# First rows turned in four operations, first weights in halves, two warming matmuls less, last output rows in halves

## The chip, the core and the metric

The kernel runs on one core of a Trainium2 chip. The metric is the time of one execution on the device in microseconds (us). The span is what the profiler sees from the first to the last event on the core; the time of the execution lies a little above it. Engines are named as the profile names them: PE is TensorE, PEld its weight loads, DVE VectorE, ACT ScalarE, POOL GpSimd, SP the engine whose queue issues the DMAs.

## What is computed

The output is a gated mix of two blocks on the same input x (2048 rows of 512): `g * a + (1 - g) * b`, with one gate `g` for each row.

```python
g = sigmoid((x * gate_w).sum(-1, keepdims=True))
# A: 64 segments of 32 rows, one after the other; 8 memory rows go ahead of each
h = concatenate([mem, xs])                       # 40 rows
q, k, v = h @ Wq, h @ Wk, h @ Wv                 # 32 heads of 128
o = softmax(mask(q @ k.T * scale)) @ v @ Wo      # 40 rows of 512
mem, a_s = o[:8], o[8:]                          # the memory of the next segment, the output rows
# B: 4 spans of 512 rows, 32 heads of 16
b = (sig(beta) * phi(q) @ M / (phi(q) @ z) + (1 - sig(beta)) * causal_softmax(q, k, v)) @ wo
M, z = M + phi(k).T @ v, z + phi(k).sum()        # after each span
```

Since A's memory goes from segment to segment, its 64 segments are a serial chain; B's work is put between their steps.

## The kernel before, in words

The program is a list of operations for each engine (class `Prog`). Each engine works through its list in order; an operation names what it reads and writes, and waits on the semaphores of the operations that it depends on. PSUM has eight banks, handed out by `Banks` from a list of free ones, a bank being a resource of its own (`rbank`): an operation that reads a bank waits for the whole operation that wrote it. DMAs are issued by SP in the order of its own list, so an entry that waits holds up those behind it.

**The head.** `plan_warm` (L500) gives TensorE 9 matmuls of 128x512 on zeros (`WARM`, L12). `plan_loads` (L515) issues, in this order: x 0 (rows 0 to 511, two DMAs of 256 rows), B's wk, wq and wv (512 KB, a DMA each), x 1, beta and mem0, x 2, x 3, gate_w. The 12 DMAs of A's weights Wk, Wq and Wv come later, one after every third piece of B's projections, between the stores of these pieces. x lies for the time being in the memory of A's Wo (`Wo_sb` in the profile), and wv in `woB_sb`.

`x_chunk` (L576) turns 512 rows of x to put the contraction on the partitions. For each half of 256 rows it takes one bank, and one operation makes 8 transposes of 128x128 (L588); two copies then take the bank to `xT`, on ScalarE for the first half and on VectorE for the second (`evac`, L390 and L392). `b_projections` makes the pieces of B: `pk` (L679) is a projection of k or q, four matmuls of 128x512 over the four parts of the contraction (L686), `kn` turns k (L720), `pv` makes v (L704), `mz` adds to the state M and z (L738). Results are stored in DRAM scratch (L662: `scr_kqd`, `scr_vd`, `scr_mzd`), from where B's attention loads them again. The memory of the head's tensors is used again for A's; `over` (L368) collects which earlier operations a tensor of A must wait for. One such case is `t1_sb`, which lies over `V17` and first holds late V rows of B (L841, then a copy by ScalarE, L390).

**The middle.** A's segments and B's attention follow 16 lists of unit names written out by hand (`A_LIST0` to `A_LIST15`, four segments each). A unit's name says what it does: `3.W1a` is a product with Wo in the fourth segment of the list, `H0` and `H1` copy the two halves of the product's sum to `WF`, `F0` and `F1` add up (fold) the four row groups and turn them by matmuls against a 0/1 matrix (L1396), `ax0` and `ax1` copy the folded rows to `aT_st`. A `~` behind a name exchanges ScalarE and VectorE for that unit's copy.

**The output rows.** `tail_units` (L1468) makes the output of 128 rows (a group; there are 16): `tb` multiplies B's rows by wo (16 matmuls of 128x512 in quarters of the partitions, L1487), `tbe` scales them by 1 - g on ScalarE into `t1_sb` (L1495), `tf` and `tfe` add g times A's rows on VectorE (L1520) and store the result (L1522). For the last group, A's rows are turned by 16 matmuls against the identity (`atr`, L1511), and sum and store are made in two halves. `tl` in a list calls `tail_load` (L1755), which sets up the next group; it does so only once that group's rows of A are all written (`stored`). So the last group's units all come after the last list, in the loop at the end of `plan_a`.

Of the kernel before, what the change touches and what calls it, by code (L numbers as in the profile page):

```python
# [8 lines left out]
F32 = mybir.dt.float32  # L9

DEV = dict(nseg_limit=None)
WARM = 9  # L12


class Op:
# [242 lines left out]
def build(nc, es, A_x, A_mem0, A_Wq, A_Wk, A_Wv, A_Wo, B_wq, B_wk, B_wv, B_wo, B_beta, gate_w, out, dbg=None):  # L258
# [109 lines left out]
    def over(home):  # L368

        parts = {"mem0_sb": "mem0", "beta_sb": "beta", "gB_sb": "gB", "omgB_sb": "omgB"}  # L370
        ops = []
        for p in v.under[home]:
            p = parts.get(p, p)
            for n, r in list(R.items()):
                if n == p or p in ("V17", "phK") and n.startswith(p) or p.startswith("stgk") and n[:-1] == p:
                    ops += ([r.w] if r.w else []) + r.readers
        return list({id(o): o for o in ops}.values())
    G = {}
# [136 lines left out]
def plan_loads(v, A_x, A_mem0, A_Wq, A_Wk, A_Wv, B_wq, B_wk, B_wv, B_wo, B_beta, gate_w):  # L515
# [8 lines left out]
            o = 4 * k + 2 * h  # L524
            ld("x%d%d" % (k, h), v.x_sb[:, o:o + 2, :], xsrc[:, o:o + 2, :], "x_sb%d%d" % (k, h), "dma_x%d%d" % (k, h))
    x(0)
    for nm, dst, src in (("wk", v.wkB, B_wk), ("wq", v.wqB, B_wq), ("wv", v.wvB, B_wv)):
        ld("b" + nm, dst[:, :, :].rearrange("p (h n) m -> p h (n m)", h=2), src.rearrange("(h p n) m -> p h (n m)", h=2, n=2), nm + "B", "dma_" + nm)
    x(1)
    g = P.group("small")  # L530
    for fn, res in ((lambda s: s.dma_start(v.beta_sb[:, :], B_beta.rearrange("(o n) -> o n", o=1).to_broadcast([128, v.HB])), "beta"),
# [44 lines left out]
def x_chunk(v, k):  # L576

    P, Rs, BK, C = v.P, v.Rs, v.BK, v.C
    for h in range(2):
        bk = BK.take()  # L580
        tiles = (4 * k + 2 * h, 4 * k + 2 * h + 1)

        def f(pe, bk=bk, tiles=tiles):
            ins = None
            for n, i in enumerate(tiles):
                for c in range(C):
                    o = (n * C + c) * 128
                    ins = pe.transpose(v.pb16[bk][:, o:o + 128], by_pairs(v.x_sb[:, i, :])[:, c, :], v.ident[:, :])  # L588
            return ins
        P.op("pe", f, reads=[Rs("x_sb%d%d" % (k, h)), Rs("ident")], writes=[v.rbank[bk]], name="xtr%d_%d" % (k, h))  # L590
        t0 = 128 * tiles[0]
        dst = v.xT[:, :, t0:t0 + 256].rearrange("p c (n t) -> p n c t", t=128)
        src = v.pb16[bk][:, 0:1024].rearrange("p (n c t) -> p n c t", n=2, c=C)
        for n in range(2):
            v.evac("dve" if h else "act", dst[:, n, :, :], src[:, n, :, :], [bk], [Rs("xT%d_%d%d" % (k, h, n))], "xev%d_%d%d" % (k, h, n))
        BK.give(bk)


def x_res(v, k):
# [49 lines left out]
def b_projections(v):  # L649
# [29 lines left out]
    def pk(sb, f, m):  # L679
        w, wr = (v.wkB, "wkB") if m == "k" else (v.wqB, "wqB")  # L680
        bk = BK.take()

        def fp(pe):
            ins = None
            for c in range(C):
                ins = pe.matmul(v.pb[bk], w[:, c, f * 128:(f + 1) * 128], v.xT[:, c, 512 * sb:512 * (sb + 1)], start=(c == 0), stop=(c == C - 1))  # L686
            return ins
        P.op("pe", fp, reads=x_res(v, sb) + [Rs(wr)], writes=[v.rbank[bk]], name="p%s%d_%d" % (m, sb, f))
        stage = v.stgk[f][:, "kq".index(m), :]
        rs = Rs("stgk%d%s" % (f, m))  # L690
        v.evac("dve" if m == "k" and f < 3 else "act", stage, v.pb[bk], [bk], [rs], "ev%s%d_%d" % (m, sb, f))
        BK.give(bk)
        if m == "k":
            return
        store("stk%d_%d" % (sb, f), v.kqd[sb, f], v.stgk[f][:, :, :], [Rs("stgk%dk" % f), rs], [Rs("kqd%d_%d" % (sb, f))], "stk%d_%d" % (sb, f), "stk%d" % f)
# [159 lines left out]
class BAttn:  # L855
# [394 lines left out]
    2.V0x 2.V0y 2.v1 2.Y0 2.n1 2.M0 2.N1 2.PV1 2.v0~ 2.L0 2.PL1 2.E1a 2.E1b tb 2.N0 2.PV0 2.n0 2.PL0 2.E0b 2.W1a tbe tf 2.W1b 2.W0b 2.E0a~ 2.W0a 2.oL pl0x  # L1250
    2.H0 2.H1 2.F0 2.hm0 pl0 2.F1 2.hm1 3.K0x tfe 3.Q0x 2.ax0~ 3.Q0y 3.q0~ 3.K0y 3.k0 3.TQ0 3.K1x 3.K1y 3.Q1x tl 3.Q1y 3.TK0 3.S0 3.V0x 3.k1~ 3.q1 3.TK1
    3.X0 3.TQ1 pl1x 3.V0y 3.Y0 3.S1 3.M0 2.ax1 3.X1 tb 3.v0 3.Y1 3.L0 3.n0 tbe 3.V1x 3.M1 tf 3.N0 tfe 3.L1 3.n1 3.N1 3.PV0 3.PL0 3.E0b~ 3.E0a 3.V1y 3.v1~
    pl1 pl1e 3.W0a 3.PV1 3.PL1 3.W0b pf 3.E1b~ 3.W1b 3.E1a pfe~ 3.W1a 3.H0~ 3.H1~ tb 3.F0 3.ax0~ tbe 3.F1 3.ax1 tf tfe
    """
A_LISTS = (A_LIST0,) + (A_LIST1,) + (A_LIST2,) + (A_LIST3,) + (A_LIST4,) + (A_LIST5,) + (A_LIST6,) + (A_LIST7,) + (A_LIST8,) + (A_LIST9,) + (A_LIST10,) + (A_LIST11,) + (A_LIST12,) + (A_LIST13,) + (A_LIST14,) + (A_LIST15,)
A_ENG = dict(E0a="act", E0b="act", E1a="act", E1b="dve", H0="act", H1="act", K0="act", K1="act", KL0="dve", KL1="dve", O0="dve", O1="dve",
# [4 lines left out]
def plan_a(v, nseg):  # L1261
# [146 lines left out]
    def ol_units(g):  # L1408
# [40 lines left out]
        def turn():  # L1449
            stored.append(g)  # L1450
            flat = aT_st[par][:, :, :].rearrange("p c t -> p (c t)")
            turned = [Rs("aTl%d" % par)] + [Rs("aTx%d_%d" % (par, r)) for r in range(4)]
            P.op("dve", lambda d: d.transpose(flat.bitcast(F32), flat.bitcast(F32)), writes=turned, name="aT%d" % g)
            grp = P.group("as%d" % g, "as%d" % par)
            rows = v.aTd[g].rearrange("(b t) (h j i) -> j t h b i", b=4, h=2, j=4)
            for j in range(4):
                P.dma(grp, lambda sp, j=j: sp.dma_start(rows[j], flat[SEG * j:SEG * (j + 1), :].rearrange("p (h b i) -> p h b i", h=2, b=4)),
                      reads=turned, writes=[Rs("aTd%d" % g)], name="sta%d_%d" % (g, j))
# [9 lines left out]
    def tail_units(g):  # L1468

        last = g == ngrp - 1  # L1470
        rows = a_rows(aT_st[g % 2])
        rr = [Rs("aTl%d" % (g % 2))] + [Rs("aTx%d_%d" % (g % 2, r)) for r in range(4)] if last else [Rs("aTg")]
        if g % 4 == 0:
            b_rows(g)
        if not last:
            P.dma(P.group("al%d" % g, "al"), lambda sp: sp.dma_start(aTg[:, :, :].rearrange("p c t -> p (c t)"), v.aTd[g]), reads=[Rs("aTd%d" % g)], writes=[Rs("aTg")],
                  name="lda%d" % g, scratch=True)

        def ub():
            bb = B.take()  # L1480

            def f_(pe):
                ins = None
                for f in range(C):
                    for j in range(4):
                        q = slice(SEG * j, SEG * (j + 1))
                        ins = pe.matmul(pb[bb][q, :], oTg[:, f, q], woB_sb[:, f, :], start=(f == 0), stop=(f == C - 1))  # L1487
                return ins
            P.op("pe", f_, reads=[Rs("oTg"), Rs("woB")], writes=[rbank[bb]], name="brow%d" % g)
            if g % 4 < 3:  # L1490
                b_rows(g + 1)
            return lambda: ub2(bb)

        def ub2(bb):
            P.op("act", lambda a: a.activation(t1_sb[:, :], pb[bb], ACT.Copy, scale=omg_sb[:, g:g + 1]),  # L1495
                 reads=[rbank[bb], Rs("omg")], writes=[Rs("t1")], name="t1_%d" % g)
            B.give(bb)

        fin = aTg[:, :, :].rearrange("p c t -> p (c t)")

        def uf():
            bk = B.take()
            if not last:
                return lambda: uf2(bk)

            def f_atr(pe):
                ins = None
                for c in range(C):
                    for j in range(4):
                        q = slice(SEG * j, SEG * (j + 1))  # L1510
                        ins = pe.matmul(by_pairs(pb[bk][q, :])[:, c, :], rows[:, c // 2, q, c % 2], ident[:, :], start=True, stop=True)  # L1511
                return ins
            P.op("pe", f_atr, reads=rr + [Rs("ident")], writes=[rbank[bk]], name="atr%d" % g)
            return lambda: uf2(bk)

        def uf2(bk):
            n = 2 if last else 1
            for h in range(n):
                c = slice(h * 512 // n, (h + 1) * 512 // n)
                P.op("dve", lambda dv, c=c: dv.scalar_tensor_tensor(fin[:, c], (pb[bk] if last else fin)[:, c], g_sb[:, g:g + 1], t1_sb[:, c], ALU.mult, ALU.add),  # L1520
                     reads=([rbank[bk]] if last else [Rs("aTg")]) + [Rs("g"), Rs("t1")], writes=([Rs("aTg")] if not h else []) + ([Rs("aTg%d" % h)] if n > 1 else []), name="fin%d_%d" % (g, h))
                P.dma(g_out[g], lambda sp, c=c: sp.dma_start(out2d[g * 128:(g + 1) * 128, c], fin[:, c]), reads=[Rs("aTg%d" % h if n > 1 else "aTg")],  # L1522
                      name="out%d_%d" % (g, h))
            B.give(bk)
        return {"tb": ub, "tf": uf}

    def x_copy(s):
# [3 lines left out]
    def segment(s):  # L1531
# [152 lines left out]
        def w_rows(hf):  # L1684
            if last:
                dst = a_rows(aT_st[par])[:, :, SEG * r:SEG * (r + 1), :].rearrange("p a t c -> p a c t")
                evac(("act", "dve")[hf], dst[:, hf], folded(wb["f%d" % hf]), [wb["f%d" % hf]], [Rs("aTx%d_%d" % (par, r)), Rs("aTl%d" % par)], "atx%d_%d" % (s, hf))
                B.give(wb["f%d" % hf])
                if hf:
                    assert ended  # L1690
                    stored.append(g)
                return
            dst = a_rows(aT_st[par])[:, :, SEG * r:SEG * (r + 1) - M, :].rearrange("p a t c -> p a c t")
            evac(ENG["ax"], dst[:, hf], folded(wb["f%d" % hf])[:, :, M:SEG], [wb["f%d" % hf]], [Rs("aTx%d_%d" % (par, r))], "atx%d_%d" % (s, hf))
# [59 lines left out]

    def tail_load(units):  # L1755
        t = st["tails"]
        if t < ngrp and len(stored) > t and bat.jobs_done >= 4 * (t // 4) + 4 and "tb" not in units and "tf" not in units and "tf" not in pend:
            units.update(tail_units(t))
            st["tails"] += 1

# [99 lines left out]
```

## Time and profile before

| what | value |
|---|---|
| time, median of 3 runs (range) | 838.7 us (838.27 to 839.15) |
| the profiled execution: its own time, its span | 837.07 us, 835.4 us |
| PE busy | 807.0 us, 97% of the span |
| DVE, ACT busy | 572.8 us (69%), 596.6 us (71%) |
| POOL busy | 284.3 us (34%) |
| chain that ended last | PE 83%, ACT 7%, DVE 4%, DMA 2% |
| bytes moved by DMA | 57.48 MB, 69 GB/s in the mean |

Busy time is the time in which an engine worked on an instruction; it is not time on the critical path. The strip on the page cuts the span into 40 slices of 20.9 us and gives the busy share of each in tenths. A line of the timeline gives start, length, engine, line of the kernel, operation, what is written and read, and how many instructions were merged; in brackets stands how long the engine had been idle before and what it waited for. The ends of matmuls are modelled: of a row of matmuls, the starts are to be trusted. The chain of waits is followed back from the last instruction, at each step to what released it.

### The profile page before, as it was taken

To read this page: it belongs to the slowest core of one execution; us is meant where nothing else is said; L and a number is where in the kernel's file an instruction comes from. 1 tells how busy PE (TensorE), PEld (TensorE's weight loads), DVE (VectorE), ACT (ScalarE), POOL (GpSimd) and SP (SyncE) were. 2 spreads that over 40 slices of the span, in tenths; PEclk is the share of its full clock that TensorE was granted. 3 is DMA by queue.
4 is the path that set the end of the run, shared out by engine and by line. 5 is a ranking of instruction groups with operands and counts; after the bars stand their busy time and mean duration, and the time that the engine had idled before them with its cause. 6 is when DMAs were issued, how large, how long until landed. Compare 5 with 4: busy or idle time off the path is not lost.

```text
span 835.4 us, 49003 instructions
## 1 busy us (share of the span) xinstructions
PE 807.0 (97%) x21933; PEld 434.8 (52%) x21933; DVE 572.8 (69%) x1382; ACT 596.6 (71%) x1519; POOL 284.3 (34%) x780
## 2 busy tenths in 40 slices
PE   8998999999999999999999999999999999999998
PEld 4544455555555555555555555554555554555544
DVE  4545565677677777777776876777766777777664
ACT  5546777777777777777677787777778677787644
POOL 3603242333333333334242333333333333434210
PEclk9999999999999999999999999999999999999999
DMA  9996312112111121111101121111112111110021
GB/s 320 420 380 214 79 36 61 47 32 48 32 30 40 24 55 26 47 38 46 36 20 40 36 56 26 46 39 35 35 32 53 24 36 45 47 36 16 17 60 41
DMA packets 98225, 57.48 MB, mean 69 GB/s; under 512 B 71768, under 2 KB 92128, under 8 KB 96480
## 3 DMA queue, kind: packets, MB, share of 16 engines
q1 hardware_dynamic: 98016, 54.36, 22.4%
q8 instruction: 172, 2.82, 1.4%
q14 instruction: 37, 0.30, 0.1%
HBM read 37.14 MB, written 17.20 MB: 65 GB/s over the span
## 4 chain that ended last, share of the span: by engine, by line
PE 83%; ACT 7%; DVE 4%; DMA 2%; issue 2%; SPq 2%; POOL 0%; DVEq 0%; ACTq 0%
PE ps L1291 44%; PE ps L1378 16%; PE ps L1396 3%; PE ps L1636 3%; PE ps L686 2%; PE ps L919 2%; PE ps L972 2%; PE ps L1571 1%; PE ps L1487 1%; PE ps L1606 1%; PE ps L704 1%; ACT PT L940 1%; ACT R_sb L1616 1%; ACT WF L390 1%; DVE P_sb L1620 1%
## 5 line engine op out<-in xcount | busy, mean ns | idle before, releaser
L946 POOL TENSOR_SCALAR_AFFINE_SELECT PT<-PT 128x128 bf16<-128x128 bf16 (+2 forms) x320 | 116.5, 364 | 197.2 <-ACT PT L940 142.0
L940 ACT ACTIVATE PT<-ps 128x512 bf16<-128x512 f32 x320 | 174.5, 608 | 4.9 <-PE ps L972 3.0
L1291 PE MATMUL ps<-Wq_sb,hT 128*32 128x512 bf16 x2048 | 138.4, 379 | 0.6
L1291 PE MATMUL ps<-Wv_sb,hT 128*32 128x512 bf16 x2048 | 138.5, 379 | 0.0
L1291 PE MATMUL ps<-Wk_sb,hT 128*32 128x512 bf16 x2048 | 135.8, 379 | 0.4
L1378 PE MATMUL ps<-Wo_sb,OT_sb 128*32 128x512 bf16 x2048 | 129.4, 380 | 0.6 <-ACT OT_sb L390 0.6
L1626 POOL TENSOR_TENSOR P_sb<-P_sb,R_sb 128x64 bf16<-128x64 bf16 x128 | 50.6, 395 | 144.6 <-ACT R_sb L1616 136.2
L390 ACT ACTIVATE OT_sb<-ps 128x320 bf16<-128x320 f32 x167 | 67.0, 434 | 24.3 <-PE ps L1648 22.8
L1291 PEld LDWEIGHTS ps<-Wq_sb,hT 128*32 128x32 bf16 x2048 | 58.6, 97 | 46.4 <-ACT hT L390 3.8
L1291 PEld LDWEIGHTS ps<-Wk_sb,hT 128*32 128x32 bf16 x2048 | 58.9, 97 | 45.4 <-ACT hT L390 1.9
L390 ACT ACTIVATE WF<-ps 128x256 f32<-128x256 f32 x106 | 35.5, 381 | 55.0 <-PE ps L1378 52.8
L1303 DVE STREAM_TRANSPOSE QT_sb<-QN_sb 128x256 f32<-128x256 f32 x128 | 56.3, 440 | 26.3 <-ACT QN_sb L390 24.1
L1303 DVE STREAM_TRANSPOSE KT_sb<-KN_sb 128x256 f32<-128x256 f32 x128 | 55.8, 438 | 25.1 <-ACT KN_sb L390 22.4
L390 ACT ACTIVATE QN_sb<-ps 128x512 bf16<-128x512 f32 x85 | 50.9, 600 | 29.9 <-PE ps L1291 28.8
L1378 PEld LDWEIGHTS ps<-Wo_sb,OT_sb 128*32 128x32 bf16 x2048 | 47.4, 96 | 45.5 <-ACT OT_sb L390 7.9
L390 ACT ACTIVATE KN_sb<-ps 128x512 bf16<-128x512 f32 x82 | 49.3, 602 | 28.0 <-PE ps L1291 27.4
L1291 PEld LDWEIGHTS ps<-Wv_sb,hT 128*32 128x32 bf16 x2048 | 50.2, 95 | 27.1 <-ACT QN_sb L390 0.7
L1585 ACT ACTIVATE P_sb<-ps 128x224 bf16<-128x224 f32 x128 | 45.9, 360 | 24.9 <-PE ps L1576 14.5
L1620 DVE TENSOR_TENSOR P_sb<-P_sb,R_sb 128x160 bf16<-128x160 bf16 x128 | 42.5, 333 | 22.4 <-ACT R_sb L1616 21.2
L392 DVE CAST OT_sb<-ps 128x320 bf16<-128x320 f32 x89 | 42.1, 486 | 19.0 <-PE ps L1648 17.9
L392 DVE CAST V_sb<-ps 128x512 bf16<-128x512 f32 x75 | 51.0, 681 | 4.6 <-PE ps L1291 3.0
L1636 PEld LDWEIGHTS ps<-P_sb,V_sb 32*128 32x128 bf16 x2048 | 23.0, 91 | 57.6 <-DVE P_sb L1620 21.8
(139 smaller groups left out, 1482.9 us busy)
## 6 DMA issues: line engine op xcount, KB each, us to landing
Wk_sb<-in_A_Wk_dram SPq DMA_DIRECT2D x4, 1024.0 KB, 8.8
Wq_sb<-in_A_Wq_dram SPq DMA_DIRECT2D x4, 1024.0 KB, 12.4
Wv_sb<-in_A_Wv_dram SPq DMA_DIRECT2D x4, 1024.0 KB, 14.3
Wo_sb<-in_A_Wo_dram SPq DMA_DIRECT2D x8, 512.0 KB, 5.6
scr_vld<-VNL SPq DMA_DIRECT2D x16, 256.0 KB, 3.4
VL<-scr_vld SPq DMA_DIRECT2D x64, 64.0 KB
scr_kqd<-stgk SPq DMA_DIRECT2D x12, 256.0 KB, 8.7
Vj<-scr_vd SPq DMA_DIRECT2D x32, 68.0 KB, 2.4
```

The lines of the kernel that those rows point to most:

```text
L390: P.op("act", lambda a: a.activation(dst, src, ACT.Copy), reads=[v.rbank[k] for k in bks], writes=dres, name=name)
L392: P.op("dve", lambda d: d.tensor_copy(dst, src), reads=[v.rbank[k] for k in bks], writes=dres, name=name)
L940: P.op("act", lambda a: a.activation(pt, v.pb[bk], ACT.Exp, scale=v.SCALE_B), reads=[v.rbank[bk]], writes=[rp], name="be%d_%d" % (n, t))
L946: P.op("gp", lambda g: g.affine_select(mv, mv, [[0, len(cut)], [1, 128]], ALU.is_ge, 0.0, base=0, channel_multiplier=-1), reads=[rp], writ ...
L1291: ins = pe.matmul(pb[bk][SEG * j:SEG * (j + 1), :], lhs(c), cols(w, j) if split else w[:, 512 * j:512 * (j + 1)], start=(c == 0), stop=(c ...
L1303: P.op("dve", lambda d: d.transpose(to, src), reads=reads, writes=writes, name=name)
L1378: ins = pe.matmul(pb[bk][SEG * j:SEG * (j + 1), :], lhs(4 * k + j), Wo_sb[:, 4 * k + j, :], start=(first and k == ks[0]), stop=False, skip ...
L1396: ins = pe.matmul(pb[bk][SEG * j:SEG * (j + 1), SEG * n:SEG * (n + 1)], cols, v.fold[:, :], start=True, stop=True, skip_group_check=True)
L1585: P.op("act", lambda a: a.activation(P_sb[:, b, :], pb[bk][:, 0:224], ACT.Exp, scale=SCALE), reads=[rbank[bk]], writes=[Rs("P%d" % b), Rs( ...
L1620: P.op("dve", lambda d: d.tensor_tensor(wide(P_sb, b)[:, :, 0:L], wide(P_sb, b)[:, :, 0:L], R_sb[:, b, :].rearrange("p (i q) -> p i q", q= ...
L1626: P.op(ENG["n"], lambda d: d.tensor_tensor(left(P_sb), left(P_sb), grp04(R_sb[:, b, :]), ALU.mult), reads=[Rs("R%d" % b)], writes=[Rs("P%d ...
L1636: ins = pe.matmul(pb[bks[j]][:, L * i:L * (i + 1)], V_sb[SEG * j:SEG * (j + 1), b, i * E:(i + 1) * E], P_sb[SEG * j:SEG * (j + 1), b, LW * ...
```

## The change

1. `WARM` goes from 9 to 7.
2. `x_chunk(0)` makes four operations of 4 transposes, each with a bank of its own, and the copies go to ScalarE and VectorE in turn. The other chunks stay as they were.
3. wk and wq are loaded in two DMAs each, by halves of the contraction. The first projection of k and of q is cut into two operations that wait for one half each.
4. The last group's output rows: both B's product and the turned rows of A are made in halves of 256 columns with a bank each. The first half of B's product and its scaling are planned at `tb`, the second at `tbe`; each final sum waits for its own halves. The last segment's rows become two resources (`aTe0`, `aTe1`), of which each half of the turn waits for one.
5. The last list: `tl` and `tb` go ahead of `F0`, the two copies `H0` and `H1` and the copy `ax0` lose their `~`, and `tbe` goes behind `ax1`. `tail_load` lets the last group through at once.

```diff
-WARM = 9
+WARM = 7
...
-                if n == p or p in ("V17", "phK") and n.startswith(p) or p.startswith("stgk") and n[:-1] == p:
+                if n == p or p in ("V17", "phK", "wkB", "wqB") and n.startswith(p) or p.startswith("stgk") and n[:-1] == p:
...
-    for nm, dst, src in (("wk", v.wkB, B_wk), ("wq", v.wqB, B_wq), ("wv", v.wvB, B_wv)):
-        ld("b" + nm, dst[:, :, :].rearrange("p (h n) m -> p h (n m)", h=2), src.rearrange("(h p n) m -> p h (n m)", h=2, n=2), nm + "B", "dma_" + nm)
+    for nm, dst, src in (("wk", v.wkB, B_wk), ("wq", v.wqB, B_wq)):
+        for h in range(2):
+            ld("b%s%d" % (nm, h), dst[:, 2 * h:2 * h + 2, :].rearrange("p n m -> p (n m)"), src.rearrange("(h p n) m -> h p (n m)", h=2, n=2)[h],
+               "%sB%d" % (nm, h), "dma_%sp%d" % (nm, h))
+    ld("bwv", v.wvB[:, :, :].rearrange("p (h n) m -> p h (n m)", h=2), B_wv.rearrange("(h p n) m -> p h (n m)", h=2, n=2), "wvB", "dma_wv")
...
+    apart = k == 0
     for h in range(2):
-        bk = BK.take()
+        bks = [BK.take() for _ in range(2 if apart else 1)]
...
+        if apart:
+            for n in range(2):
+                turn((n,), bks[n], "xtr%d_%d%s" % (k, h, "xy"[n]))
+        else:
+            turn((0, 1), bks[0], "xtr%d_%d" % (k, h))
...
-            v.evac("dve" if h else "act", dst[:, n, :, :], src[:, n, :, :], [bk], [Rs("xT%d_%d%d" % (k, h, n))], "xev%d_%d%d" % (k, h, n))
-        BK.give(bk)
+            bk = bks[n % len(bks)]
+            src = v.pb16[bk][:, 0:1024].rearrange("p (n c t) -> p n c t", n=2, c=C)
+            v.evac("dve" if (n if apart else h) else "act", dst[:, n, :, :], src[:, n, :, :], [bk], [Rs("xT%d_%d%d" % (k, h, n))], "xev%d_%d%d" % (k, h, n))
+        BK.give(*bks)
...
+        cut = ((0, 1), (2, 3)) if sb == 0 and f == 0 else (range(C),)
+        for n, cs in enumerate(cut):
...
+            P.op("pe", fp, reads=x_res(v, sb) + [Rs("%s%d" % (wr, h)) for h in sorted({c // 2 for c in cs})], writes=[v.rbank[bk]],
...
-    pl1 pl1e 3.W0a 3.PV1 3.PL1 3.W0b pf 3.E1b~ 3.W1b 3.E1a pfe~ 3.W1a 3.H0~ 3.H1~ tb 3.F0 3.ax0~ tbe 3.F1 3.ax1 tf tfe
+    pl1 pl1e 3.W0a 3.PV1 3.PL1 3.W0b pf 3.E1b~ 3.W1b 3.E1a pfe~ 3.W1a 3.H0 3.H1 tl tb 3.F0 3.ax0 3.F1 3.ax1 tbe tf tfe
...
-        rr = [Rs("aTl%d" % (g % 2))] + [Rs("aTx%d_%d" % (g % 2, r)) for r in range(4)] if last else [Rs("aTg")]
+        rr = [Rs("aTl%d" % (g % 2))] + [Rs("aTx%d_%d" % (g % 2, r)) for r in range(3)]
...
+            brow(0)
+            if last:
+                t_rows(0, bbs[0])
             if g % 4 < 3:
                 b_rows(g + 1)
-            return lambda: ub2(bb)
+            return lambda: ub2(bbs, brow)
...
+        def t_rows(h, bb):
+            c = slice(512 // n * h, 512 // n * (h + 1))
+            P.op("act", lambda a: a.activation(t1_sb[:, c], pb[bb][:, c], ACT.Copy, scale=omg_sb[:, g:g + 1]),
+                 reads=[rbank[bb], Rs("omg")], writes=[Rs("t1")] if not h else [Rs("t1b")], name="%s%d_%d" % ("th" if last else "t1_", g, h))
+
+        def ub2(bbs, brow):
+            if last:
+                brow(1)
+            t_rows(n - 1, bbs[n - 1])
+            B.give(*bbs)
...
+                P.op("pe", f_atr, reads=rr + [Rs("aTe%d" % h), Rs("ident")], writes=[rbank[bks[h]]], name="atrh%d_%d" % (g, h))
...
-        if t < ngrp and len(stored) > t and bat.jobs_done >= 4 * (t // 4) + 4 and "tb" not in units and "tf" not in units and "tf" not in pend:
+        if t < ngrp and (t == ngrp - 1 or len(stored) > t) and bat.jobs_done >= 4 * (t // 4) + 4 and "tb" not in units and "tf" not in units and "tf" not in pend:
```

## The prediction

> **What bounds the kernel.** I read the utilisation strip of the page first, then the timeline of the two ends, then the chain of waits between them, because the change works only in the first 11 us and the last 6 us.
>
> ```profile
> PE   8998999999999999999999999999999999999998
> ...
> DMA  9996312112111121111101121111112111110021
> ```
>
> TensorE is busy nearly everywhere (807.0 of 835.4 us), but in the first three slices (a slice is 20.9 us) the 16 DMA engines are full as well. So a gain on TensorE at the start need not last until the end. The timeline of the head:
>
> ```profile
> 1.26 4.02 PE L509 MATMUL ps<-WF 128*128 128x512 bf16 x9 [1.26 <-DVE WF L503]
> ...
> 5.08 1.91 PE L588 MATMUL ps<-ident,Wo_sb 128*128 128x128 bf16 x16
> ...
> 6.17 1.09 ACT L390 ACTIVATE xT<-ps 128x512 bf16<-128x512 bf16 x2 [4.09 <-PE ps L588]
> 7.03 0.76 DVE L392 COPY xT<-ps 128x512 bf16<-128x512 bf16 x2 [5.82 <-PE ps L588]
> ...
> 7.89 1.02 PE L686 MATMUL ps<-xT,wkB 128*128 128x512 bf16 x4 [0.90 <-DVE xT L392]
> ...
> 9.15 1.04 PE L686 MATMUL ps<-xT,wqB 128*128 128x512 bf16 x4 [0.23 <-DMA wqB<-in_B_wq_dram]
> ```
>
> Columns are start, length, instructions, and in brackets the idle time before and its releaser. Nine warming matmuls, sixteen transposes, then the projections; the second projection waits for wq, and from 9.15 on TensorE has work without a gap to 48.7. The chain of waits further on:
>
> ```profile
> 53.45 0.53 SPq L662
> ...
> 55.06 3.56 DMA scr_vd<-V
> 58.62 2.12 issue
> 60.74 0.26 POOL t_sb L841
> 61.00 0.02 issue
> 61.02 0.05 ACT t_sb L390
> ```
>
> Here the chain leaves TensorE: V stores leave SP's queue, land, GpSimd's memset of the reused tile (L841) waits for them, and ScalarE, in order, stands idle 2.77 us behind it. VectorE too waits then, for the store of MZ (until 61.13). What paces SP is seen in two issues of the same store:
>
> ```profile
> 10.85 0.35 SPq L662 DMA_DIRECT2D scr_kqd<-stgk  x1
> ...
> 49.29 1.92 SPq L662 DMA_DIRECT2D scr_kqd<-stgk  x1
> ```
>
> An issue that took 0.35 takes 1.92 later: the queue is full, and the DMA share between 50 and 61 is 0.98 to 1.15. The V copies whose stores leave at 52.98 to 55.5 began at 45.93 to 48.72. So this place is set by the transfers, not by TensorE. The end:
>
> ```profile
> 829.52 0.76 DVE L392 COPY WF<-ps 128x256 f32<-128x256 f32 x2 [1.42 <-PE ps L1378]
> 830.00 0.55 PEld L1396 LDWEIGHTS ps<-fold,WF 128*32 128x32 f32 x32 [1.01 <-DVE WF L392]
> 830.00 0.67 PE L1396 MATMUL ps<-fold,WF 128*32 128x32 f32 x32 [0.52 <-DVE WF L392]
> 830.41 0.57 DVE L392 CAST aT_st<-ps 128x64 bf16<-128x64 f32 x2
> ...
> 830.48 1.05 PE L1487 MATMUL ps<-woB_sb,oTg 128*32 128x512 bf16 x16
> ...
> 831.35 0.62 PE L1511 MATMUL ps<-ident,aT_st 128*32 128x128 bf16 x16
> 831.57 0.69 ACT L1495 ACTIVATE t_sb<-ps,omg_sb 128x512 f32<-128x512 f32 x1 [2.52 <-PE ps L1487]
> 832.35 0.88 DVE L1520 SCALAR_TENSOR_TENSOR aTg<-ps,g_sb,t_sb 128x256 bf16<-128x256 f32 x2 [1.37 <-ACT t_sb L1495]
> ```
>
> This is serial: copy, fold, B's rows, ScalarE's scaling, two final sums to 833.23, and 2.17 us for the last store to 835.4.
>
> **The head, step by step.** Two warming matmuls less: starts are 0.427 apart (4.22 to 4.65), so the transposes start 0.85 earlier, at 4.23. The earliest x load took 2.7 us to land (0.81 + 2.7 = 3.5); the second half of x is not needed before 5.08. Sixteen transposes at 0.107 (1.71 for 16) then run 4.23 to 5.94, results some 0.2 later. Four operations with a bank each let each copy start after four transposes: ScalarE takes tiles 0 and 2 (pitch 0.5 of L390), VectorE 1 and 3 (0.38). The last copy starts near 6.2 and ends near 6.6, against 7.79: 1.2 earlier.
>
> The weights then decide. wk was issued at 1.80 and landed 6.0 later, at 7.80; wq was issued at 2.31 and landed at 9.10. As halves they are the same packets in the same order, but each issue costs SP 0.47 + 0.04, so the last half of wq is issued at 3.34, 1.03 later. Its landing is not in this trace. From below, the queue is the limit and it lands at 9.1 or a little before, since wv comes behind it later too; from above, landing moves with the issue, 10.13. I take 9.1, because the next load (wv, issued at 2.83) landed at 10.4: each 512 KB comes 1.3 us after the one before though issued 0.5 apart, so bytes set the pace. After it only two matmuls of that projection are left, not four: 2 x 0.216 = 0.43 gained. With the ends: 0.6 lost to 1.0 gained on TensorE at 10 us.
>
> SP's other entries (wv, x 1, beta, mem0, x 2, x 3, gate_w) go 1.03 later. x 1's second half was issued at 3.9; even with the longest landing of any x load, 8.2, and 1.03 more it is there at 13.1, and is turned at 13.92, or 13.5 with the gain. The last entry ends at 10.37 instead of 9.34, and the first store at SP would come at 10.4: no loss. DMA does not run dry: x 3, issued by 8.29, takes some 8 us to land. The new names for reuse of memory add only operations that ended long before: nothing.
>
> **Where the 0.43 goes.** It reaches 48.7, and then the V stores at 53 to 55.5, which stand behind a full queue. Bytes and their order are unchanged, so the release at 61.02 stays; the cover is the DMA backlog. In the other direction TensorE has slack too: the projection that ScalarE copies at 61.02 (L823 at 55.64 and 59.12) ended at 59.7 and the V projection that VectorE copies at 61.13 at 60.15, so a lag of 1.0 to 1.3 us is swallowed as well. I put the head at 0, with 0.5 lost to 1.0 gained as ends.
>
> **The tail.** (a) The two copies of the sum's halves go from VectorE to ScalarE: 0.39 to the first fold on ScalarE's row at 817.83 against 0.44 for VectorE: 0.04 gained, F0 near 829.96. ScalarE is free from 829.05. (b) The first half of B's rows goes ahead of the folds: 16 matmuls of 256 columns. Sixteen of 512 take 0.87 (830.48 to 831.35), so 0.44; TensorE's last product starts at 829.08 to 829.3, so they run 829.3 to 829.75 in the 0.52 gap. Were the gap gone, 0.44 would come back. Behind them waits F0, which has until 829.96. (c) th0 on ScalarE after both copies (they take 0.66: 830.18) takes about 0.38, the 128x256 row's time, to 830.56; queued behind it is the copy of fold 0, to 830.8; VectorE copies fold 1 by about the same time. (d) Second half of B's rows behind the folds: 830.37 to 830.81, results 831.0; th1 831.0 to 831.4. (e) The turned rows: eight matmuls at 0.02 (16 in 0.62, of which 0.3 is one's own latency), 830.85 to 831.2; the other half just behind. (f) Final sums: 831.25, and the second, after th1, ends by 832.15, against 833.23. The last store follows with its 2.17. **Sum: 1.1 us less.** If the wider pieces do not overlap as I lay them, only the halving of the 0.70 scaling is left, 0.4; at best the whole 0.78 from scaling to sum, the 0.44 and the 0.04 go, 1.3.
>
> **The warm clock, a rule against the change.** Warming matmuls and transposes ran at half the later pitch (0.427 and 0.107 against 0.216 and 0.055), and the first projection, at 7.89, at full pitch, though the granted clock reads 1.00 in all of these. So the rate rose between 6.8 and 7.9, that is 5.5 to 6.6 us after the first matmul. The Trainium skill (TensorE: Matmul & The Clock Gate, Part 1 and Part 4) has the gate open after about 3.4 us of sustained work and says that transposes do not count. By that rule, seven matmuls (an estimate of 3.0 us) would leave it shut; it would open 3.4 us into the projections, cost 1.7 us there, and after the slack 0 to 0.3 would be left: 837.6 to 837.9.
>
> **The rivals.**
> 1. *The head's gain lasts.* If the release at 61 is partly TensorE's after all, 0.4 to 1.0 more comes: 836.6 to 837.2. For it: TensorE has no wait on a transfer between 9.2 and 55. Against it: the full queue. 0.27.
> 2. *Slower: the rate rises late.* If only the projections count towards it, from about 7.0, it rises up to 6.6 us later, at 13.6, and half rate until then costs 3.3. Less 0.4 of the head and 1.0 to 1.3 of slack, 1.6 to 1.9 reach the end; less 1.1, that is 0.5 to 0.8 slower: 839.4. It ends slower than before when the rise comes after about 12.4 us: half of 12.4 - 7.0 is 2.7, the 0.4, the slack of 1.2 and the tail's 1.1 together. Against it: 5 us of other work come first. 0.07.
> 3. *The tail does not overlap*, for instance because B's first half is not placed ahead of the folds: 0.4 at most, 838.3. 0.11.
> Forecast, 0.55: the head at 0, the tail at 1.1.
>
> **Numbers.** The profiled execution took 837.07 (span 835.4 and 1.67 around it); I expect 835.97 there, span 834.3. The median shown, 838.7, lies 1.63 above that execution, so I apply the difference: 837.6. The range takes in the head's ends and the third rival, with the 0.45 that runs lie about their median (838.27 to 839.15): 836.4 to 839.1; outside are the second rival and the best of the first. A measurement of this kernel can tell some 0.2%, 1.7 us, from no change. Faster by more than that needs the better half of the first rival, 0.14, or the forecast with the runs' spread, 0.04: 0.18. Slower by more needs the second rival beyond its estimate: 0.04. Within: 0.78.
>
> **What would show it.** Transposes at 4.2, the last copy of xT at 6.6, the second half of wq between 9.1 and 10.1, TensorE 0.4 earlier near 48, and still a release of ScalarE near 61.0; then L1487 in two groups, one before the folds, and final sums that end 2.7 us after the last Wo product (829.5) instead of 3.7. I am wrong if the release at 61 moves, if projections after 7 us run at 0.427, or if the last store starts no earlier.

## The result, and the profile after

The kernel after takes 836.33 us in the median (834.67 to 838.26, 12 runs), the kernel before, run beside it, 838.75 (836.93 to 843.1, 12 runs). The ratio is 0.9968, with a 95% interval from 0.9954 to 0.9981: 2.7 us less (1.6 to 3.9). Forecast were 837.6 and a range from 836.4 to 839.1. The profiled execution took 835.59 with a span of 833.9; before it was 837.07 and 835.4.

The strip of the page is the same picture as before, full transfers in the first three slices included:

```profile
PE   8998999999999999999999999999999999999998
...
DMA  8997312112111111112101121111112012110121
```

The timeline of the head (start, length, instructions; in brackets the idle time and its releaser):

```profile
4.22 1.46 PE L593 MATMUL ps<-ident,Wo_sb 128*128 128x128 bf16 x16
4.89 1.20 ACT L390 ACTIVATE xT<-ps 128x512 bf16<-128x512 bf16 x2 [2.79 <-PE ps L593]
5.27 0.87 DVE L392 COPY xT<-ps 128x512 bf16<-128x512 bf16 x2 [4.07 <-PE ps L593]
6.56 1.19 PE L699 MATMUL ps<-xT,wkB 128*128 128x512 bf16 x4 [0.88 <-DMA wkB<-in_B_wk_dram]
7.79 1.26 PE L699 MATMUL ps<-xT,wqB 128*128 128x512 bf16 x4
8.44 0.12 PEld L699 LDWEIGHTS ps<-xT,wqB 128*128 128x128 bf16 x2 [0.54 <-DMA wqB<-in_B_wq_dram]
8.89 1.03 PE L699 MATMUL ps<-xT,wkB 128*128 128x512 bf16 x4
```

The transposes start at 4.22. The last copy of xT ends at 6.14. The first halves of wk and wq are there for 6.56 and 7.79, and the last half of wq for 8.44. From the third projection on TensorE is 1.13 ahead (8.89 against 10.02). The chain of waits further on:

```profile
29.55 15.70 DMA scr_kqd<-stgk
...
45.33 0.10 ACT stgk L390
...
55.93 2.97 DMA scr_vd<-V
...
60.76 0.03 ACT t_sb L390
```

The release of ScalarE comes at 60.76 (61.02 before). The first row of this chain is new to the reader: a store issued at 29.55 lands 15.7 later, and ScalarE's copy into the same staging place waits for it until 45.33. In the kernel before, the same copy also waited for a store, and started at 44.48:

```profile
44.48 0.60 ACT L390 ACTIVATE stgk<-ps 128x512 bf16<-128x512 f32 x1 [1.99 <-DMA scr_kqd<-stgk]
```

So TensorE's lead of 1.13 is gone by 45 us. The end of the kernel after:

```profile
828.89 0.62 PE L1505 MATMUL ps<-woB_sb,oTg 128*32 128x256 bf16 x16
...
829.55 0.61 PE L1410 MATMUL ps<-fold,WF 128*32 128x32 f32 x32
829.66 0.48 ACT L1517 ACTIVATE t_sb<-ps,omg_sb 128x256 f32<-128x256 f32 x1
829.98 0.62 PE L1505 MATMUL ps<-woB_sb,oTg 128*32 128x256 bf16 x16
...
830.64 0.47 ACT L1517 ACTIVATE t_sb<-ps,omg_sb 128x256 f32<-128x256 f32 x1 [0.37 <-PE ps L1505]
830.86 0.88 DVE L1546 SCALAR_TENSOR_TENSOR aTg<-ps,g_sb,t_sb 128x256 bf16<-128x256 f32 x2 [0.39 <-PE ps L1538]
```

B's first half (L1505) lies ahead of the folds, the second between them and the turned rows. From the first copy to `WF` to the end of the span it is 4.78 (829.12 to 833.9); before it was 5.88 (829.52 to 835.4). That is 1.1 less.

So 1.1 of the 2.7 us lie in the tail, as forecast, and some 1.6 elsewhere, where the forecast had nothing. The two profiled executions show only 0.4 of these 1.6 (the first copy to `WF` at 829.12 in place of 829.52). The experiments are about the 1.6.

### The profile page after: what moved, and what is told of

Same layout as the page of the kernel before. It is cut to its first block, busy times and chain, and to the rows that moved or that the text cites. A ratio compares the mean times of both kernels' runs of the same rounds, so it can differ in the third digit from the quotient of the medians.

```text
span 833.9 us, 49027 instructions
## 1 busy us (share of the span) xinstructions
PE 805.4 (97%) x21941; PEld 433.5 (52%) x21947; DVE 571.7 (69%) x1379; ACT 597.1 (72%) x1523; POOL 284.2 (34%) x780
## 4 chain that ended last, share of the span: by engine, by line
PE 80%; ACT 8%; DMA 5%; DVE 4%; issue 2%; SPq 1%; POOL 0%; DVEq 0%; ACTq 0%
PE ps L1305 44%; PE ps L1392 16%; PE ps L1410 3%; PE ps L1663 3%; PE ps L933 2%; PE ps L986 2%; DMA scr_kqd<-stgk 2%; PE ps L1598 1%; PE ps L699 1%; PE ps L1505 1%; PE ps L1633 1%; ACT R_sb L1643 1%; ACT PT L954 1%; ACT WF L390 1%; DVE P_sb L1647 1%
```

## The experiments

Each set of runs was made on one chip, with the kernel before beside it. The medians of the kernel before go from 837.2 to 840.8 from set to set, so only ratios within a set are compared. Single runs of one kernel in a set spread over 2 to 8 us; a ratio of 12 runs has an interval of about 1.3 us to each side (e5 and e7 have 6 runs, e15 8, e13 11). The ratio isn't the quotient of the two medians in the table; in e1 the two differ. A range called resampled comes from drawing the runs of each kernel anew, with replacement.

Each run also has the clock granted to TensorE on record, as a mean over its span. In the profiled executions this mean is 0.998 or 0.997 for just the seven whose trace shows the clock at one half for 3.41 us within the work (e2, e6, e8, e10, e11, e13, e17), and 0.999 or 1.000 for all others. So it counts such falls in the runs without a trace too: below, a run lost clock when its mean is 0.998 or less, and what it lost is the missing share of its span.

Theory 1: the transfers swallow all of the head; only the tail's 1.1 counts. Theory 2: part of the head's lead lasts.

| run | kernel | time, us | before, us | ratio, 95% interval |
|---|---|---|---|---|
| e1_head | parts 1 to 3 | 836.56 | 837.18 | 0.9973 (0.9956 to 0.9991) |
| e2_tail | parts 4 and 5 | 837.55 | 837.18 | 1.0002 (0.9987 to 1.0017) |
| e3_after_again | after | 835.35 | 837.18 | 0.9976 (0.9961 to 0.9991) |
| e4_before_again | before | 838.33 | 837.18 | 1.0005 (0.9989 to 1.0020) |
| e5_warm12 | after, 12 warming matmuls | 835.74 | 839.56 | 0.9953 (0.9939 to 0.9968) |
| e6_light_before | before, 1 MB less | 837.79 | 839.56 | 0.9985 (0.9969 to 1.0000) |
| e7_light_after | after, 1 MB less | 835.37 | 839.56 | 0.9955 (0.9939 to 0.9972) |
| e8_stage3 | after, three staging places | 838.61 | 839.56 | 0.9987 (0.9974 to 0.9999) |
| e9_halves | part 3 | 839.82 | 839.60 | 1.0005 (0.9990 to 1.0020) |
| e10_turns | parts 1 and 2 | 839.83 | 839.60 | 1.0003 (0.9988 to 1.0018) |
| e11_early_wk | before, A's loads earlier | 839.89 | 839.60 | 1.0005 (0.9985 to 1.0024) |
| e12_late_wk | after, A's loads later | 838.24 | 839.60 | 0.9978 (0.9964 to 0.9993) |
| e13_after_third | after | 837.56 | 840.75 | 0.9964 (0.9945 to 0.9984) |
| e14_fill6 | after, TensorE held by 6 matmuls | 836.96 | 840.75 | 0.9955 (0.9940 to 0.9971) |
| e15_fill12 | after, TensorE held by 12 | 836.56 | 840.75 | 0.9959 (0.9939 to 0.9979) |
| e16_keepwarm | before, idle time filled | 839.03 | 840.75 | 0.9980 (0.9965 to 0.9995) |
| e17_turns_again | parts 1 and 2 | 840.11 | 839.23 | 1.0011 (0.9997 to 1.0024) |
| e18_turns_warm | e17, idle time filled | 838.98 | 839.23 | 0.9998 (0.9987 to 1.0009) |

### Head and tail apart (e1 to e4)

e1 has the head of the change and the old tail, e2 the reverse. e3 and e4 are the kernels after and before, unchanged.

```diff
 e1: -WARM = 9
     +WARM = 7          and parts 2 and 3; list, tail_units, w_rows, tail_load as before
 e2: parts 4 and 5      and WARM, plan_loads, x_chunk, pk as before
```

> Parts 1 to 3 of the change alone (7 warming matmuls, four turning operations, halves of wk and wq); the output rows as before. Theory 1 (the lead of the head is used up by waits for transfers between 40 and 61 us): within 0.5 us of before, and ScalarE's release near 61 not moved with the head. Theory 2 (part of the lead lasts, and is what the change brought beyond the tail's 1.1): 0.9 to 1.6 us faster than before.

> Parts 4 and 5 alone (last output rows in halves, first half of B's product ahead of the folds). Theory 1: 1.1 us faster than before, and the first 820 us of the trace as before. Theory 2: also 1.1, and the rest of the measured 2.4 in the head. Rival of both (the tail is worth more than its trace shows): 2.0 or more.

> The changed kernel once more, unaltered, for a second trace and a second comparison on the chip that runs the two parts. Theory 1: 1.1 to 1.5 us faster than before, the larger figure of the first comparison being spread. Theory 2: 2.0 to 2.7 us faster, the sum of the two parts.

> The kernel before once more, unaltered, for a second trace of it and to see how far two equal programs differ. Both theories: no difference. If ScalarE's release near 61 us lies elsewhere than 61.0 here (by 0.5 us or more), the transfers set it anew in each execution, and one pair of traces can't measure the middle.

By the ratio the head alone gives 2.3 us (0.8 to 3.7), which theory 1 doesn't allow; the medians lie only 0.6 apart, the means 1.6. e3 repeats the whole change: 2.0 (0.8 to 3.3). e4, an unchanged kernel, comes out at 1.0005, which shows what such a ratio can tell. The tail alone gives nothing in time (1.1 faster to 1.4 slower), though its trace has the shorter tail: 4.76 from the first copy to `WF` to the end. The same trace shows a part of what hid it. TensorE waits 1.38 up to 75.57, and from 77.1 on the granted clock is at one half (view by windows: stretch; its length with the busy time and count of PE, PEld, DVE, ACT and POOL; then granted clock, DMA share, GB/s):

```profile
76.00:78.00 2.00, 1.77 (x44) 0.77 (x40) 1.72 (x4) 1.32 (x4) 0.00 (x0) 0.78 0.58 194
78.00:80.00 2.00, 2.00 (x28) 0.90 (x24) 0.48 (x1) 0.81 (x2) 0.00 (x0) 0.50 0.42 150
80.00:82.00 2.00, 1.70 (x44) 0.78 (x36) 1.40 (x4) 0.92 (x4) 0.00 (x0) 0.86 0.43 96
```

What is missing to 1.00 adds up to 2 x (0.22 + 0.50 + 0.14) = 1.7 us. By the clocks on record six of e2's 12 runs had such a fall, and 7 of the 35 of the kernel before: some 0.7 us more clock lost in the mean, against the tail's 1.1.

### The lead and the bytes (e5 to e8)

```diff
 e5: -WARM = 7
     +WARM = 12
 e6, e7 (on before, on after), plan_loads: the fourth part of Wv isn't loaded
     -        for c in range(C):
     +        for c in range(C - (res == "Wv")):
 e8 (on after), late V rows: three staging places in place of one
     -        self.vst = v.t1_sb...
     +        self.vst = [(t1, ["t1"]), (wf, ["warm", "WF0", "WF1"]), (ot, ["oTt"]), (t1, ["t1"])]
```

> The changed kernel with 12 warming matmuls instead of 7: the halves, the four operations and the tail stay, but the lead of TensorE at the third projection (10.02 before, 8.89 after) is put back to about 10.0. Theory 1 (only the tail's 1.1 is certain, the lead is used up at the full queue by 45 us): as the changed kernel, 1.1 faster than before. Theory 2 (the lead lets SP issue the weight loads earlier, the transfers get ahead, and part of it lasts to 80 us): the head's gain is lost, some 1.2 us slower than the changed kernel.

> The kernel before without the load of the fourth part of Wv (1 MB; A's V projections use the third part twice, so V is not the reference's). Transfers set the time from 40 to 80 us (both theories): fold 0 of the first segment, at 79.7 before, comes 1 to 2.4 us earlier, and so does the end. Rival (TensorE or ScalarE sets it): no earlier than before by more than 0.3.

> The changed kernel without the same load (V again not the reference's). Theory 1: the head counts for nothing as long as transfers lie behind it; against the light kernel before, the end gains the tail's 1.1 and at most 0.5 more. Theory 2: with the queue relieved, the lead of 1.1 lasts in full: 2.0 us or more against the light kernel before.

> The changed kernel, with three places in SBUF for the late V rows of B instead of one, so that the copies le1 to le3 need not wait until the store before has landed. Theory: between 61 and 80 us the time is set by that chain of store and copy, whose links wait behind Wo's loads; then the first fold comes 1 us or more earlier than in the changed kernel (79.6), and the end too. Rival (the chain only looks like it; the loads of VL and Wo are late anyway): within 0.5 us of the changed kernel.

Five warming matmuls more cost nothing that shows, but they delayed the third projection by 0.27 only (9.16 in place of 8.89), not to 10.0 as was planned, so this says little on the lead. 1 MB less brings ScalarE's release to 59.37 in e7 (60.76 with it), so that place can follow the bytes; in e6, whose trace has a fall of the clock in the head, it is at 62.06. In time 1 MB less brings the kernel before 1.3 us (0 to 2.6). Between the two light kernels lie 2.4 us, theory 2's figure; but e6 lost clock in 6 of its 12 runs and e7 in none of 6, and among the runs at 1.000 the medians differ by 1.8. e8 failed on its own terms: TensorE waits 2.67 up to 80.77 for a place that is still being stored, and its clock falls to 0.50 behind that wait too.

### Which part of the head (e9 to e12)

```diff
 e9: part 3 alone; e10: parts 1 and 2 alone
 e11 (on before), where A's 12 weight loads are planned
     -        if weights and n % 3 == 2:
     +        if weights and n % 3 == 0:
 e12 (on after)
     -        if weights and n % 3 == 2:
     +        if weights and n % 3 == 2 and n > 2:
```

> The kernel before with part 3 alone (wk and wq in halves, first projections cut). In both runs of the kernel before, the first store leaves SP at 10.55 to 10.85; in the runs with the whole head at 9.5 to 10.1. Theory 2 (the head's gain lasts because SP can issue the first stores, and behind them the first loads of A's Wk, earlier, so that the full-queue stretch begins earlier) expects the gain with the halves: with nine warming matmuls and two banks, the copies of xT end at 7.8 as before, wq's second half is there by then, the first store leaves near 10.1, and the time is 0.5 to 1.0 below the kernel before. Theory 1 (the transfers swallow all of the head) expects no difference (0.3 either way).

> The kernel before with parts 1 and 2 alone (seven warming matmuls, four turning operations with a bank each; wk and wq whole). The second projection waits for wq as a whole, which landed at 8.4 to 9.1 in the runs of the kernel before, whatever TensorE does. Theory 2 expects that the first store leaves as in the kernel before (10.2 to 10.9) and that nothing is gained (0.3 either way). A rival within theory 2, that the earlier start of TensorE itself is what lasts, expects 1 us less. Theory 1 expects 0.

> The kernel before with nothing of the change, but with all 12 loads of A's Wk, Wq and Wv planned two pieces earlier, so that the first one leaves SP ahead of the first store, near 9.4 in place of 11.2. TensorE's work and its starts are those of before. If the start of the big loads is what lasts (theory 2 with the transfers), this alone gives 1 to 2 us, and the release of ScalarE near 61 comes 0.5 to 1 earlier. If what lasts is TensorE's or the stores' lead, it gives nothing, or loses some tenths because each store now stands behind a load: 0 to 0.5 slower.

> The kernel after with all 12 loads of A's weights planned three pieces later (the first one leaves SP behind the second store or the third, near 12 in place of 10.1); the head's lead on TensorE is kept. If the start of the big loads is what lasts, the head's gain is lost and 1 us more: 837 to 839 where the kernel before stands at 838.3 (no gain beyond the tail's 1.1, or less). If TensorE's lead is what lasts, the time stays that of the kernel after, 835.5 to 836.5 on that scale.

All three single causes fail. Halves alone give nothing; turns alone give nothing; the big loads 1.8 us earlier (9.40 in place of 11.24) give nothing; and with the big loads 2.0 later (12.11) the kernel after keeps 1.8 us (0.6 to 3.0). So it isn't the start of A's loads by itself.

But e10, e11 and e6 have something in their traces that no trace with the whole new head has. TensorE is idle ahead of the first projection for 2.72, 2.13 and 2.29, and the first two projections then run for the most part at 0.427 a matmul in place of 0.216, with the granted clock at 0.50. In e11:

```profile
4.73 1.06 PE L588 MATMUL ps<-ident,Wo_sb 128*128 128x128 bf16 x16
7.92 1.87 PE L686 MATMUL ps<-xT,wkB 128*128 128x512 bf16 x4 [2.13 <-DMA wkB<-in_B_wk_dram]
```

The kernel before, whose rows stand in the prediction, got wk at nearly the same time (7.80). What differs is the transposes: at full pitch (0.056) in e11 and done at 5.8, at half pitch (0.107) in the kernel before and done at 7.0. Theory 3: in part of its executions the older head loses TensorE's clock while it waits for wk, and the new head ends this.

### Delay of TensorE, and loss of its clock (e13 to e18)

```diff
 e14, e15 (on after), pk, ahead of the third projection; 6 and 12 matmuls
     +        if sb == 0 and f == 1 and m == "k":
     +            P.op("pe", lambda pe: [pe.matmul(v.pb[bk], v.warm[:, 0:128], v.warm[:, :], start=True, stop=True) for _ in range(12)][-1],
     +                 reads=[Rs("warm")], writes=[v.rbank[bk]], name="fill")
 e16 (on before): the same with f == 0 and range(4), that is ahead of the first projection
 e18 (on e10): the same with f == 0 and range(8)
```

> The kernel after once more, unchanged, as the base of the next two, and for its time on one more set of runs. All theories: 2 to 4 us under the kernel before of the same set; TensorE idle for less than 1.1 us ahead of the first projection, and every projection at full pitch.

> The kernel after with six more matmuls of 128x512 on zeros ahead of the third projection (the first of wk's second column). At 0.216 each that moves TensorE's row of projections from there on by 1.3 us, with the transfers' order and the first store as they were; the third projection starts near 10.1, where it started in the two fast heads of the kernel before. Theory 1 (the transfers swallow a shift of this size): 0 to 0.3 slower than the kernel after. Theory 3 (the start of the steady row of projections counts in full at any place): 1.3 slower. A bent curve, which the releases of ScalarE so far suggest (60.2 to 60.9 for starts of the third projection between 8.7 and 9.7, 61.0 for 10.0, 62.7 for 11.0): 0.3 to 0.6 slower.

> The same with twelve: 2.6 us. The third projection starts near 11.4, as in the executions of the older head in which the first two projections ran at half pitch (11.0 to 11.4). Theory 1 with the slack of 1.0 to 1.3: 1.3 to 1.6 slower than the kernel after, release of ScalarE near 62.2. Theory 3 in full: 2.6 slower. The bent curve: 1.7 to 2.0 slower, release near 62.7.

> The kernel before with four more matmuls of 128x512 on zeros between the transposes and the first projection, and nothing of the change. In three traces with the older head TensorE stood idle there for 2.1 to 2.7 us, and the first two projections ran at 0.427 a matmul, not 0.216 (third projection 11.0 to 11.4); in the traces with up to 1.8 us of idle time they ran at 0.216 (9.3 to 10.0). The four take 0.9 of the idle time away. Theory 3 (the loss of the pitch in part of the executions is what the new head ends): 0.4 to 1.0 below the kernel before, projections at full pitch in the trace, and fewer of the slowest times. Theories 1 and 2: no difference.

A delay of TensorE alone costs nothing that can be measured here: the medians of e14 and e15 lie 0.6 and 1.0 below that of e13 (e15 less e13, resampled: 2.2 less to 1.7 more). In e15 the third projection is 2.66 later than in the kernel after, and the first store of results and the first load of Wk are where they were (9.78 and 10.17). The copy that waits for the staging place starts at 45.82, not at 45.33 + 2.66:

```profile
8.96 2.75 PE L694 MATMUL ps<-WF 128*128 128x512 bf16 x12
11.55 1.03 PE L702 MATMUL ps<-xT,wkB 128*128 128x512 bf16 x4
```

```profile
45.82 0.60 ACT L390 ACTIVATE stgk<-ps 128x512 bf16<-128x512 f32 x1 [1.81 <-DMA scr_kqd<-stgk]
```

ScalarE's release is at 61.36, 0.6 later than in the kernel after. That is theory 1, and it speaks against the bent curve of the expectation, by which 1.7 to 2.0 were due, though 1.7 lies at the very edge of what the runs allow. But e16, which is the kernel before with four matmuls more and no other change, is 1.7 us faster (0.4 to 2.9) than the kernel before. It lost clock in 4 of its 12 runs, the kernel before in 17 of 30; that is 0.5 us less in the mean, not all of the 1.7. The last two runs differ in such a filling alone:

> The kernel of e10 once more (parts 1 and 2 alone), as the base of the next. In e10 its transposes ended at 5.15, TensorE then stood idle for 2.72 us, and the granted clock read 0.50 between 8 and 10 us, a loss of 1.7 us in all. All theories: the same dip in this trace.

> The same kernel with eight matmuls of 128x512 on zeros between the transposes and the first projection: at 0.216 they fill 1.7 of the 2.7 us, the data that the projections wait for lands as before. Expected in the trace: idle time of 1.0 there, no dip, first store near 10.3 in place of 11.8. If the loss of 1.7 us in the head reaches the end (theory 3), this is 1.2 to 1.7 us faster than e17. If the transfers swallow it, as the delays of e14 and e15 were swallowed (theory 1), the two are within 0.5 us.

e17, timeline of TensorE, and the view by windows with the columns named above:

```profile
7.95 1.65 PE L694 MATMUL ps<-xT,wkB 128*128 128x512 bf16 x4 [2.39 <-DMA wkB<-in_B_wk_dram]
9.39 1.91 PE L694 MATMUL ps<-xT,wqB 128*128 128x512 bf16 x4
```

```profile
6.00:8.00 2.00, 0.05 (x1) 0.08 (x2) 0.01 (x1) 0.00 (x0) 0.13 (x1) 1.00 0.94 306
8.00:10.00 2.00, 2.00 (x6) 0.71 (x7) 0.36 (x1) 0.00 (x0) 0.00 (x0) 0.55 1.03 378
10.00:12.00 2.00, 2.00 (x7) 0.70 (x5) 0.33 (x1) 0.60 (x1) 0.00 (x0) 0.60 0.96 310
```

e18, the same two views:

```profile
8.03 1.02 PE L697 MATMUL ps<-xT,wkB 128*128 128x512 bf16 x4
```

```profile
8.00:10.00 2.00, 1.73 (x8) 0.68 (x9) 0.69 (x1) 0.00 (x0) 0.00 (x0) 1.00 1.01 350
```

e17 stands idle for 2.39, loses 2 x (0.45 + 0.40) = 1.7 us of clock, and its first store leaves at 11.96. e18 begins the first projection 0.08 later, at full clock, and its first store leaves at 10.98. ScalarE's release comes at 63.52 and 62.30. The medians are 840.11 and 838.98: the loss of clock costs 1.1 us at the end (resampled, 0.1 to 2.3). It is the rule in one kernel and the exception in the other: by the clocks on record e17 lost clock in 11 of its 12 runs, e18 in 2, a difference of 1.7 us in the mean. The 1.1 lies between the two theories, slightly below theory 3's 1.2 to 1.7.

e15 and e17 are reconciled by what SP does. In e15 the delay lies behind the first store, so 1 MB of Wk is issued at 10.17 and the transfers work through the delay. In e17 the delay lies ahead of it: the first Wk load goes at 12.36 (e18: 11.38), by 20 us 5.63 MB are moved (e18: 6.16; after: 6.34; e15: 6.19), and at 45 us the gap between e17 and e18 is still 0.57 MB. At the 0.42 MB per us of that stretch this is 1.4 us, and the releases are 1.2 apart. That the missing bytes carry the delay is read from these traces; no run changed the bytes of the first 20 us alone.

## Why the prediction was wrong, point by point

**The tail: right.** 1.1 was forecast, 1.1 is read from the traces of after, e2 (4.76) and e3 (4.71), by the steps as laid: B's first half ahead of the folds, th0 behind the two copies, B's second half between the folds and the turned rows. Only th0 took 0.48, not 0.38. In time it can't be told apart: e2 came out at no change.

**The head's own steps: right in order, too careful in size.** Transposes at 4.2 held; the last copy of xT ended at 6.14, not 6.6; the last half of wq was there for 8.44, ahead of both bounds (9.1 and 10.13), since the halves landed 4.6 to 5.1 after issue in this trace, where a whole one took 6.0 to 6.8 in that of before. The lead was 1.13, not 0.43. But that is one pair of traces: without a fall of the clock the third projection started between 9.33 and 10.02 with the older head (before, e2, e4) and between 8.69 and 9.55 with the new one (after, e1, e3, e7, e8, e12, e13).

**The failed step: "I put the head at 0", from "Where the 0.43 goes".** This term of the sum was about 1.5 us too small. The kernel after stands 2.6 us below the kernel before (mean of 0.9968, 0.9976 and 0.9964, an interval of some 0.8 to each side), and the tail has 1.1 of that. The mechanism of the step was right for one kind of shift: a delay of TensorE behind the first store is swallowed, even one of 2.7 us (e15), and earlier than I said, by the staging copies at 39 to 45, where TensorE itself shows no long wait. What the step left out is that the older head isn't the same in each execution. The one that I read happened to wait 0.90 ahead of the first projection. Of seven traces with whole wk and wq and no filling, four waited 2.1 to 2.7 and lost 1.7 us of clock; of the kernel with the old head as it was (before, e2, e4, e6, e11) it is two of five. With the whole new head the wait was at most 1.3 in ten traces, and none lost its clock there, since the first projection, with half of wk, could begin at 6.3 to 7.2 (7.4 in e5, behind its warming matmuls), where with the whole of wk it began at 7.2 to 8.1.

**Is that all of it?** No, it is the smaller part. By the clocks on record 55 of the 146 runs of the kernel before in the five sets lost clock, and 9 of 35 of the kernel after. In the two sets where both were run it is 7 of 35 against 1 of 12 and 17 of 30 against 5 of 11, a difference of 0.2 and 0.3 us of clock in the mean. And the runs that lost none show the gain as well: the medians of the runs at 1.000 are 837.10 and 835.07 in the set of e3 (2.0 apart; resampled, 0.9 to 3.0) and 840.12 and 836.16 in that of e13 (4.0; 1.0 to 5.9). So the clock brings some 0.3 of the 2.6 us and the tail 1.1; about 1.2 us of the head (0.4 to 2.0) stay without a shown cause. The traces don't settle it either: the first copy to `WF` starts at 79.14, 78.59 and 77.62 in after, e3 and e1, and at 79.25 and 79.48 in before and e4.

Why the parts don't add up can be said in part. The turned rows alone end the transposes earlier, while the whole of wk lands when it did; so the wait grows, and e10 and e17 lost clock in 20 of their 24 runs (the kernel before beside them in 22 of 58). The halves take that wait away: with them as well (e1) it is 2 of 12. The tail alone (e2) met more falls than the kernel beside it, as said above. There is a second place for falls, at 72 to 84 us: e2, e8 and e13 lost 1.7 us of clock there behind waits of 1.38, 2.67 and 2.08, while waits of 1.49 (e9) and 1.78 (e18) had no such loss. At which of the two places the runs without a trace lost their clock isn't on record.

**The rivals.** The first (the head's gain lasts, 0.27) comes nearest (836.6 to 837.2; 836.33 came); that the release at 61 is partly TensorE's, as it supposed, isn't shown: the release moved by 0.26 in the one pair (60.76 against 61.02), and a delay of 2.66 moved it by 0.6. The second set half a rate in the new head, where no trace has it; it is the older head that met it. The third didn't come.

**The clock rule.** The weighing came out for the trace: seven matmuls and the transposes were enough, and the first projection ran at full pitch in all ten traces of the new head. When the rate rose differs from trace to trace: in e14 and e15 by 4.2, ahead of the first transposes, in the kernel after half-way through them, at about 5.0, and in the kernel before only behind them. The four falls in the head came 3.4 us after the rise: from the spacing of the starts I put the rise at 3.95, 4.37, 4.47 and 4.79 in e10, e11, e6 and e17 (estimates), and the granted clock is at one half from 7.38, 7.78, 7.87 and 8.20, each time for 3.41 us. The Trainium skill (TensorE: Matmul & The Clock Gate, Part 1) says that the gate watches a window of about 3.4 us that runs on its own, whatever the kernel does, and halves the rate after an idle one. The 1.7 us lost in each dip, which is 3.4 us at one half, agree, and so do the 3.4 us from rise to fall and the chance in it. The idle time does not: waits of 1.4 to 2.7 us were enough here, where the page speaks of a whole window.

**The range.** It rested on three runs within 0.45 of their median. Twelve runs of one kernel spread over 3.5 us or more, and the kernel before alone moved by 3.6 us from set to set. Its low end isn't the sum of the parts that it names either: 837.6 less the head's 1.0 and the runs' 0.45 is 836.15, not 836.4.

## What to carry to other kernels

One trace is one draw. Where an engine waits for a load near its start, ask how the time goes if the work ahead of the wait ends 1 us sooner, above all whether TensorE then stands long enough to lose its clock. And before one such loss is made the cause of a difference, count it in all runs: here the granted clock of each run was on record, and runs without any loss differed as much. A few matmuls on zeros in such a wait kept the clock in the head of e16 and e18, and neither was slower for it. A delay of compute in front of a full DMA queue was free here as far as the runs can tell where the next big load was already issued (e15), and a start of these loads 0.98 later went with 1.1 us at the end (e17 against e18).

## What the runs showed of the hardware

A fall of the granted clock has nearly a fixed price in clock: 1.7 us in e2, e6, e8, e10, e11, e13 and e17, after idle times from 1.38 to 2.72. In time the runs of the kernel before with 0.998 or less took 1.2 to 2.0 us more in the mean than those at 1.000, in each of the five sets. In the head every wait of 2.13 or more brought it and none of 1.79 or less; at 75 to 82 us one of 1.38 did (e2) and one of 1.78 did not (e18).

A store of 256 KB that was issued near 30 us, behind 1 MB loads, took 13.0 to 16.0 us to land in the traces whose chain shows it; those that were issued in the first 14 us took 4.0 to 9.4.
